# A decode kernel's single rows on fewer partitions, and ten small loads that nothing reads

## The chip, the core and the metric

The kernel runs on one core of a Trainium2 chip. Five engines work at once, each through its own list of instructions in order: TensorE (PE, with its weight loads PEld), VectorE (DVE), ScalarE (ACT), GpSimd (POOL) and SyncE (SP). Sixteen DMA engines move data between HBM and the on-chip memory; SP, ScalarE and GpSimd can issue transfers to them. The metric is the device time of one execution in microseconds.

## The reference

One token is decoded by an attention block with a cache of 32 heads, 4096 keys and 128 columns, and, beside it, by a gated feed-forward layer of 1376 hidden units. Both read the same normalized row `xn` of 512 numbers:

```python
xn = layernorm(x)
q = (xn @ wq).reshape(32 heads, 128)
p = softmax(q @ k_cache^T / sqrt(128))
a = (p @ v_cache).reshape(4096) @ wo
y = (silu(xn @ w_gate) * (xn @ w_up)) @ w_down * sigmoid(xn @ w_r)
out = x + a + xn + y
```

All of it is fp32. The two caches are 64 MB each; `wq` and `wo` are 8 MB, the three feed-forward matrices 2.7 MB each. Nothing is used twice.

## The kernel before, in words

The caches are worked off in eight groups of four heads. A group's keys and its values are 8 MB each, 64 KB on each of 128 partitions. Three regions take them in turn: `ring` holds three slots of half a group (and, beyond, some space for the feed-forward matrices), `vals` holds a whole group.

For each group DVE and POOL multiply the keys by q and add up along the columns (`multiply`, `sums`, `rest`; lines 253, 264, 269, 271), PE and DVE take the maximum of a head over the partitions, ScalarE takes the exponential (line 337), POOL spreads it into `PT[g % 2]` (line 339), and PE multiplies it with the values (line 348). In the loop over g (line 432 on) the keys of group g are loaded ahead of the values of group g-1, so that transfers run beside the work on the group before. At the end come `w_down`, and `wo` in parts that get smaller and smaller, so that little is left to do when the last one lands.

SP issues nearly all transfers, in the order of the program: `wq` (line 84), the single rows (line 133), the keys of group 0 (K0) into `vals`, the two halves of `w_gate` and the two of `w_up` (line 93), then, each when its place is free, K1, V0, K2, V1 and so on. ScalarE issues two loads of 2 KB at the start, x and `w_r` (lines 129 and 130). GpSimd issues none.

`w_down` has 1376 rows. The last 1344 are laid over 128 partitions in one piece (line 123). The first 32, the single rows, have a tile of their own, `WF` (lines 132 and 133): one row of 2 KB on each of 32 partitions, in an order that makes 4 (`FEW`) the leading dimension of the source. `ffn_hidden` (line 290 on) makes the hidden units, lays the first 32 beside the others as one more block of 32 columns in `hr`, transposes, and takes `HF`, one column of 32 units, from the result. `rows_down` (line 399 on) multiplies `HF` with `WF` in one matmul (line 405) behind those with the other rows. `q_part(0)` (line 283) makes the q of the first four groups: a matmul on PE and, as its last step, a copy on ScalarE (line 245). `PT[1]` is first written at group 1.

What sets the order of the work around the change is the framework's planner. Each engine's own order is that of the program (`manual_schedule`, line 69). The planner lays these orders side by side in one list, and counts the completions of transfers that SP and ScalarE issue on eight counters, handed out in turn along that list. A transfer whose counter has had an owner waits, on the engine that issues it, until that owner has landed, beside its waits for data. In the program as it was built before, the list begins so (number of the counter, and the former owner that is waited for):

```
x 0 | wq 1 | w_r 2 | single rows 3 | K0 4
... ScalarE's copy of q_part(0) (line 245)
w_gate, first half 5 | ... | w_gate, second half 6 | w_up, first half 7
w_up, second half 0 (x) | K1 1 (wq) | V0 2 (w_r) | K2 3 (single rows)
```

The first half of `w_gate` stands directly behind ScalarE's copy of line 245, and directly ahead of POOL's and DVE's first work on K0. GpSimd's transfers have counters of their own.

Of the kernel before, what the change touches and what calls it, by code (L numbers as in the profile page):

```python
# [8 lines left out]
F32 = mybir.dt.float32  # L9
AF = mybir.ActivationFunctionType  # L10
ALU = mybir.AluOpType
# [10 lines left out]
PARTS = (16,), (8, 4, 2.5, 1, 0.5)  # L22
T = 32
FEW = 4


@with_exitstack
def kernel(
# [13 lines left out]
    nc = tc.nc  # L42
    _, H, Sk, Dh = k_cache.shape
    D = x.shape[-1]
# [14 lines left out]
    NS = -(-QR // NCOL)  # L59
# [10 lines left out]
    const = ctx.enter_context(tc.tile_pool(name="const", bufs=1))  # L70
# [12 lines left out]
    def load_wq(t):  # L83
        nc.sync.dma_start(t, wq.rearrange("(p j) n -> p (j n)", p=P))  # L84

        return [
            t[:, j * H * Dh:(j + 1) * H * Dh].rearrange("p (b h k n) -> p b h k n", b=NB, h=HP, n=QC)
            for j in range(NK)
        ]
# [16 lines left out]
    def load_keys(g):  # L106

        i = (1 - g % 2) * SLOT
        t = load_group(k_cache, g, ring[:, i:i + 2 * SLOT] if g else vals)
        t = [t[:, :HC], t[:, HC:]]  # L110
        return [(h, t[h]) for h in ((1, 0) if g % 2 else (0, 1))]
# [17 lines left out]
    nc.scalar.dma_start(xr, x[0])  # L129
    nc.scalar.dma_start(wr, w_r.rearrange("(o n) -> o n", o=1))  # L130
    WQ = load_wq(ring[:, :2 * SLOT])
    WF = const.tile([T, D], F32, name="wf")
    nc.sync.dma_start(WF, w_down[:T].rearrange("(b a) n -> a b n", a=FEW))  # L133
    K, V = {0: load_keys(0)}, {}


# [42 lines left out]
    PT = [const.tile([P, C, HP], F32, name=f"pt{i}") for i in range(2)]  # L179
# [17 lines left out]
    for j in range(NK):  # L197
        nc.tensor.matmul(ps[:, j:j + 1], xn.rearrange("o (p j) -> o j p", j=NK)[:, j], ones[0:1, 0:1],  # L198
                         start=True, stop=True)
# [3 lines left out]
    def sigmoid(z, shape, name):  # L203
        e = const.tile(shape, F32, name=name)
        nc.scalar.activation(e, z, AF.Exp, scale=-1.0)
        nc.vector.tensor_scalar(e, e, 1.0, None, op0=ALU.add)
        nc.vector.reciprocal(e, e)
        return e
# [7 lines left out]
    sr = sigmoid(ps[:, 0:1], [P, 1], "sr")  # L216

    base = const.tile([1, D], F32, name="base")
# [5 lines left out]
    for j in range(NK):  # L224
        for i in range(NQ * HP):
# [3 lines left out]
                             start=(j == 0), stop=(j == NK - 1), skip_group_check=True)  # L229
# [7 lines left out]
    late = [ring[:, SLOTS * SLOT + i * D:SLOTS * SLOT + (i + 1) * D] for i in range(MORE // D)]  # L237

    def q_part(k):

        ps = ps_q.tile([P, QB, Dh], F32, name="q")
        nc.tensor.matmul(ps.rearrange("p g d -> p (g d)"), pick.rearrange("p i h -> p (i h)"), q_sb[:, k, :],
                         start=True, stop=True)

        nc.scalar.activation(q_sb[:, k, :], ps.rearrange("p g d -> p (g d)"), AF.Copy)
        return ps
# [4 lines left out]
    def multiply(g, i, c0, c1):  # L251
        q, k = Q[g // QB][:, g % QB, :], K[g][i][1]
        nc.vector.tensor_tensor(  # L253
            k[:, c0:c1, :], k[:, c0:c1, :],
            q[:, None, :].to_broadcast([P, c1 - c0, Dh]), op=ALU.mult
        )
# [9 lines left out]
    def rest(g, i):  # L266

        k, q = K[g][i][1][:, HC - NP:], q_sb[:, g // QB, :].rearrange("p (g d) -> p g d", d=Dh)[:, g % QB, :]
        nc.gpsimd.tensor_tensor(k, k, q[:, None, :].to_broadcast([P, NP, Dh]), op=ALU.mult)  # L269
        a, b = k[:, :, :Dh // 2], k[:, :, Dh // 2:]  # L270
        nc.gpsimd.tensor_tensor(a, a, b, op=ALU.add)  # L271


    def ffn_in(W, ps):

        for j in range(NK):
            for t in range(NCOL):
                a = 0 if t == 0 else T
                nc.tensor.matmul(ps[32 * t:32 * t + 1, a:T + FT], xnT[:, j:j + 1], W[j][:, t * FT + a:T + (t + 1) * FT],  # L279
                                 start=(j == 0), stop=(j == NK - 1), skip_group_check=True)  # L280
        return ps[:, :T + FT]

    Q = {0: q_part(0)}

    rest(0, 0)
    multiply(0, 0, 0, HC - NP)
    sums(0, 0)
    gate, up = ffn_in(W_GATE, ps_acc), ffn_in(W_UP, ps_o)

    def ffn_hidden():  # L290

        hid = sigmoid(gate, [P, T + FT], "hid")
        nc.vector.tensor_tensor(hid, hid, gate, op=ALU.mult)
        hr = late[3][:, :(NS + 2) * T].rearrange("p (s i) -> p s i", i=T)
        nc.vector.memset(hr[:, :NS + 1], 0.0)
        nc.vector.scalar_tensor_tensor(
            hr[:, NS + 1].rearrange("p (a b) -> p a b", a=FEW), hid[:, :T].rearrange("p (b a) -> p a b", a=FEW), sr,
            up[:, :T].rearrange("p (b a) -> p a b", a=FEW), op0=ALU.mult, op1=ALU.mult,
        )
        for a in range(HP):  # L300
            n = min(NS + 1, QR - OFF[a])
            nc.vector.scalar_tensor_tensor(
                hr.rearrange("p s (v a) -> p a s v", a=HP)[:, a, :n],
                hid[:, T:].rearrange("p (v r) -> p r v", r=QR)[:, OFF[a]:OFF[a] + n], sr,
                up[:, T:].rearrange("p (v r) -> p r v", r=QR)[:, OFF[a]:OFF[a] + n], op0=ALU.mult, op1=ALU.mult,
            )
        hT = late[4][:, :(NS + 2) * T].rearrange("p (s i) -> p s i", i=T)
        nc.vector.transpose(hT.rearrange("p s i -> p (s i)"), hr.rearrange("p s i -> p (s i)"))
        HL = const.tile([P, NS, 2, HP], F32, name="HL")
        for w in range(2):  # L310
            nc.vector.tensor_tensor(HL[:, :, w, :], hT[:, w:w + NS, 0:1].to_broadcast([P, NS, HP]),
                                    mine[:, None, :].to_broadcast([P, NS, HP]), op=ALU.mult)
        HF = const.tile([T, 1], F32, name="HF")
        nc.vector.tensor_copy(HF, hT[:T, NS + 1, 0:1])
        return HL, HF


# [81 lines left out]
    def rows_down():  # L399

        for s in range(NS):
            t, a, b = 32 * (s % NCOL), s * D, min((s + 1) * D, FP)
            nc.tensor.matmul(down[t:t + 2 * HP, :b - a], HL[:, s].rearrange("p w a -> p (w a)"), WD[:, a:b],
                             start=(s < NCOL), stop=(s >= NS - NCOL and t > 0), skip_group_check=True)
        nc.tensor.matmul(down[0:1, :], HF, WF, start=False, stop=True, skip_group_check=True)
        sb = small.tile([P, D], F32, name="sb")
        nc.scalar.activation(sb, down, AF.Copy)
        return sb
# [16 lines left out]
    def direct(lhsT, rhs, last=False):  # L425

        for j in range(NCOL):
            nc.tensor.matmul(fin(j), lhsT, rhs[:, j * DC:(j + 1) * DC],  # L428
                             start=False, stop=last, skip_group_check=True)


    for g in range(NG + 1):
# [3 lines left out]
        elif g:  # L436
# [6 lines left out]
            down = ps_q.tile([P, QB, Dh], F32, name="q").rearrange("p g d -> p (g d)")  # L443
# [5 lines left out]
        n = (HC - NP) // 2  # L449
# [17 lines left out]
        if g:  # L467
            values(g - 1)
            keep(g - 1)
            if g == 1:  # L470
                HL, HF = ffn_hidden()
            if g == NG:
                sb = rows_down()
            if g % GB == 0:
                DEN[g // GB - 1] = collect(g // GB - 1)
# [4 lines left out]
    n = len(rows) - RB + PARTS[1][0]  # L480
# [7 lines left out]
    for j, (lhsT, rhs) in enumerate(rows[n:]):  # L488
        if j == PARTS[1][1]:
            gather(sb, first[:, 0, 0, 0:1])  # L490
        direct(lhsT, rhs, last=(rhs is rows[-1][1]))
    res = const.tile([1, D], F32, name="res")
    for j in range(NCOL):
        to = res[:, j * DC:(j + 1) * DC]
        if j % 2:
# [32 lines left out]
```

## Time and profile before

| what | value |
|---|---|
| time, median of 2 runs | 376.82 us (376.81 to 376.84) |
| span of the profiled execution, first to last instruction | 375.2 us |
| bytes read from HBM | 159.45 MB |
| mean rate over the span | 425 GB/s |
| DMA packets | 3826, of them 455 under 512 B |
| mean granted clock of TensorE | 0.686 |

The time of the profiled execution itself is not given beside its span; the two runs agree to 0.03 us, and the span is 1.6 us shorter than their median.

How to read the views quoted below. The page's first part has the busy time of each engine and its share of the span; its second part cuts the span in 40 slices and gives the busy share in tenths; its third has the DMA queues with packets, megabytes and share of 16 engines; its fourth follows the chain of work that ended last back through whatever released each step. The timeline has start, duration, engine, line, operation, what is written and read, and in brackets the idle time before and what ended it. SPq and ACTq are issues of transfers. The DMA view of a stretch gives its busy share and GB/s in 40 slices; a packet is counted where it starts. Packets under 512 B are, before the change, completion marks: one from each DMA engine that took part in a transfer.

### The profile page before, as it was taken

How to read it: one execution, taken by the hardware profiler on the slowest of the kernel's cores; microseconds unless marked ns; L12 is line 12 of the kernel's file. 1: busy time of each engine (PE TensorE's matmuls, PEld its weight loads, DVE VectorE, ACT ScalarE, POOL GpSimd, SP SyncE). 2: the span in 40 equal slices, each digit the busy share in tenths (PEclk: the TensorE clock that was granted, in tenths of full speed). 3: DMA queues.
4: the chain of work that ended last, by engine and by line, in shares of the span. 5: the costliest groups of instructions: out<-in, count | busy, mean ns of one | idle time of the engine just before them, and what ended most of it. 6: DMA issues, size and time to landing. Idle time of an engine off the chain costs nothing.

```text
span 375.2 us, 2071 instructions
## 1 busy us (share of the span) xinstructions
PE 117.0 (31%) x850; PEld 34.7 (9%) x850; DVE 228.4 (61%) x132; ACT 16.1 (4%) x37; POOL 172.1 (46%) x56
## 2 busy tenths in 40 slices
PE   1155052000810074006400480037002700180996
PEld 1111010000200011001100130001000200020222
DVE  6300499389867990699059924995399419970020
ACT  3001000000010000100000000000000000010001
POOL 2000497089307940696059704980299019910000
PEclk9999567555775559555955596558555865586799
DMA  8999899999999999999999999999999999998995
GB/s 336 447 454 447 363 462 442 447 447 426 433 412 413 447 449 426 447 440 426 433 412 433 447 442 426 447 440 421 426 434 433 447 419 433 447 435 387 441 416 226
DMA packets 3826, 159.57 MB, mean 425 GB/s; under 512 B 455, under 2 KB 583, under 8 KB 874
## 3 DMA queue, kind: packets, MB, share of 16 engines
q1 hardware_dynamic: 3814, 159.45, 98.5%
q8 instruction: 6, 0.10, 0.1%
q14 instruction: 2, 0.02, 0.0%
q10 hardware_dynamic: 4, 0.00, 0.0%
HBM read 159.45 MB, written 0.00 MB: 425 GB/s over the span
## 4 chain that ended last, share of the span: by engine, by line
DMA 74%; PE 17%; DVE 7%; SPq 1%; issue 0%; ACTq 0%; ACT 0%; DVEq 0%
DMA vals<-in_A_v_cache_dram 54%; PE ps_pv L348 17%; DMA vals<-in_A_k_cache_dram 11%; DMA ring<-in_A_wo_dram 9%; DVE s L264 4%; DVE vals L253 3%; SPq L133 0%; PE ps_acc L428 0%; SPq L118 0%; PE ps_small L324 0%; SPq L84 0%; ACTq L523 0%; ACT res L496 0%; DVE nm L329 0%; PE ps_o L428 0%
## 5 line engine op out<-in xcount | busy, mean ns | idle before, releaser
L269 POOL TENSOR_TENSOR ring<-ring,q_sb 128x3072 f32<-128x3072 f32 x14 | 93.6, 6683 | 116.4 <-DMA ring<-in_A_k_cache_dram 116.4
L348 PE MATMUL ps_pv<-vals,pt 128*16 128x512 f32 x448 | 63.8, 734 | 187.3 <-DMA vals<-in_A_v_cache_dram 187.3
L253 DVE TENSOR_TENSOR ring<-ring,q 128x2560 f32<-128x2560 f32 (+1 forms) x21 | 77.8, 3703 | 71.4 <-DMA ring<-in_A_k_cache_dram 71.4
L264 DVE TENSOR_REDUCE s<-ring 128x40 f32<-128x5120 f32 (+1 forms) x28 | 100.0, 3614 | 0.8
L271 POOL TENSOR_TENSOR ring<-ring 128x1536 f32<-128x1536 f32 x14 | 48.1, 3435 | 1.1
L348 PEld LDWEIGHTS ps_pv<-vals,pt 128*16 128x16 f32 x448 | 15.1, 113 | 231.1 <-issue 231.1
L269 POOL TENSOR_TENSOR vals<-vals,q_sb 128x3072 f32<-128x3072 f32 x2 | 13.4, 6708 | 37.7 <-DMA vals<-in_A_k_cache_dram 37.7
L253 DVE TENSOR_TENSOR vals<-vals,q 128x5120 f32<-128x5120 f32 x2 | 11.0, 5483 | 28.4 <-DMA vals<-in_A_k_cache_dram 28.4
L373 DVE RECIPROCAL rinv<-ps_small 128x4 f32<-128x4 f32 x2 | 0.4, 178 | 23.2 <-PE ps_small L364 23.2
L264 DVE TENSOR_REDUCE s<-vals 128x40 f32<-128x5120 f32 (+1 forms) x4 | 14.3, 3614 | 0.1
L357 ACT ACTIVATE pv<-ps_pv 128x512 f32<-128x512 f32 x8 | 4.8, 597 | 193.9 <-PE ps_pv L348 193.9
L348 PE MATMUL ps_pv<-ring,pt 128*16 128x512 f32 x64 | 9.3, 746 | 10.3 <-DMA ring<-in_A_v_cache_dram 10.3
L227 PE MATMUL ps_pv<-ring,xnT 128*1 128x512 f32 x64 | 8.8, 712 | 10.5 <-DMA ring<-in_A_wq_dram 10.5
L339 POOL TENSOR_TENSOR pt<-e,mine 128x512 f32<-128x512 f32 x8 | 8.3, 1040 | 7.9 <-ACT e L337 7.9
L279 PE MATMUL ps_acc<-ring,xnT 128*1 128x336 f32 (+1 forms) x32 | 4.9, 766 | 16.5 <-DMA ring<-in_B_w_gate_dram 16.5
L324 PE MATMUL ps_small<-dg,same 128*128 128x32 f32 x16 | 3.6, 309 | 18.1 <-DVE dg L322 18.1
L337 ACT ACTIVATE e<-s,nm 128x128 f32<-128x128 f32 x8 | 3.2, 402 | 119.3 <-DVE nm L329 119.3
L366 PE MATMUL ps_o<-pv,first 128*128 128x512 f32 x16 | 7.4, 604 | 0.4 <-ACT pv L357 0.4
L271 POOL TENSOR_TENSOR vals<-vals 128x1536 f32<-128x1536 f32 x2 | 6.9, 3444 | 0.2
L324 PEld LDWEIGHTS ps_small<-dg,same 128*128 128x128 f32 x16 | 2.9, 218 | 24.4 <-issue 14.9
L198 PE MATMUL ps_small<-ones,pv 1*128 1x1 f32 x8 | 2.0, 370 | 8.3 <-DVE pv L194 8.3
L375 DVE TENSOR_TENSOR ring<-ps_o,rinv 128x512 f32<-128x512 f32 x2 | 2.1, 1058 | 3.4 <-PE ps_o L366 3.4
(106 smaller groups left out, 82.5 us busy)
## 6 DMA issues: line engine op xcount, KB each, us to landing
vals<-in_A_wo_dram SPq DMA_DIRECT2D x1, 4096.0 KB, 26.4
ring<-in_B_w_gate_dram SPq DMA_DIRECT2D x2, 1376.0 KB, 44.7
ring<-in_B_w_up_dram SPq DMA_DIRECT2D x2, 1376.0 KB
vals<-in_B_w_down_dram SPq DMA_DIRECT2D x1, 2688.0 KB
ring<-in_A_wo_dram SPq DMA_DIRECT2D x1, 2048.0 KB
ring<-in_A_wo_dram SPq DMA_DIRECT2D x1, 1024.0 KB
ring<-in_A_wo_dram SPq DMA_DIRECT2D x1, 640.0 KB, 34.2
ring<-in_A_wo_dram SPq DMA_DIRECT2D x1, 256.0 KB, 34.3
```

The costliest lines, as they stand in the source:

```text
L227: nc.tensor.matmul(ps_pv[i // NCOL][32 * t:32 * t + 1, :QC], xnT[:, j:j + 1], WQ[j][:, k * QB // GB, i % HP, k % (GB // QB), :], start=(j ...
L253: nc.vector.tensor_tensor(k[:, c0:c1, :], k[:, c0:c1, :], q[:, None, :].to_broadcast([P, c1 - c0, Dh]), op=ALU.mult)
L264: nc.vector.tensor_reduce(s[:, c], k[:, c, :n], axis=AX.X, op=ALU.add)
L269: nc.gpsimd.tensor_tensor(k, k, q[:, None, :].to_broadcast([P, NP, Dh]), op=ALU.mult)
L271: nc.gpsimd.tensor_tensor(a, a, b, op=ALU.add)
L279: nc.tensor.matmul(ps[32 * t:32 * t + 1, a:T + FT], xnT[:, j:j + 1], W[j][:, t * FT + a:T + (t + 1) * FT], start=(j == 0), stop=(j == NK - ...
L324: nc.tensor.matmul(ps[:, :PP], same.rearrange("p i h -> p (i h)"), dg, start=True, stop=True)
L337: nc.scalar.activation(e, s, AF.Exp, bias=nm, scale=SCALE, accum_out=RS[g // GB][:, g % GB:g % GB + 1])
L339: nc.gpsimd.tensor_tensor(PT[g % 2], e[:, :, None].to_broadcast([P, C, HP]), mine[:, None, :].to_broadcast([P, C, HP]), op=ALU.mult)
L348: nc.tensor.matmul(ps[r:r + M, :], p[:, G * i:G * (i + 1), :].rearrange("p c h -> p (c h)"), v[:, G * i:G * (i + 1), :].rearrange("p c d - ...
L357: nc.scalar.activation(PV[g // GB][:, :, g % GB, :], ps_pv[g % 2].rearrange("p (c d) -> p c d", c=G), AF.Copy)
L366: nc.tensor.matmul(ps_o, first[:, c].rearrange("p h i -> p (h i)"), pv[:, c].rearrange("p k d -> p (k d)"), start=(c == 0), stop=(c == G - 1))
```

## The change

The single rows go onto 16 partitions, two consecutive rows (4 KB) on each; the leading dimension of the source stays 4. `hr` and `hT` get one more block of 32 columns, the first 32 units are laid as two blocks of 16, `HF` becomes two columns of 16 units, and two matmuls over 16 rows take the place of one over 32. The result row `res` uses the tile `base`, which has been read by then, instead of its own. And behind `q_part(0)` ScalarE issues seven loads of 5 to 11 rows of 128 B, GpSimd three of 5, 5 and 4 rows of 256, 192 and 160 B, all from `wo` into columns of `PT[1]` that are disjoint. Nothing reads them; `PT[1]` is overwritten as a whole at group 1.

```diff
+EACH = 2
@@ load of the single rows
-    WF = const.tile([T, D], F32, name="wf")
-    nc.sync.dma_start(WF, w_down[:T].rearrange("(b a) n -> a b n", a=FEW))
+    WF = const.tile([T // EACH, EACH * D], F32, name="wf")
+    nc.sync.dma_start(WF, w_down[:T].rearrange("(a b r) n -> a b (r n)", a=FEW, r=EACH))
@@ behind Q = {0: q_part(0)}, ahead of rest(0, 0)
+    mark, x = PT[1].rearrange("p c h -> p (c h)"), 0
+    for n in (5, 6, 7, 8, 9, 10, 11):
+        nc.scalar.dma_start(mark[:n, x:x + T], wo[16 * n:17 * n, :T])
+        x += T
+    for n, w in ((5, 64), (5, 48), (4, 40)):
+        nc.gpsimd.dma_start(mark[:n, x:x + w], wo[16 * n:17 * n, :w])
+        x += w
@@ ffn_hidden
-        hr = late[3][:, :(NS + 2) * T].rearrange("p (s i) -> p s i", i=T)
-        nc.vector.memset(hr[:, :NS + 1], 0.0)
+        hr = late[3][:, :(NS + 1 + EACH) * T].rearrange("p (s i) -> p s i", i=T)
+        nc.vector.memset(hr, 0.0)
         nc.vector.scalar_tensor_tensor(
-            hr[:, NS + 1].rearrange("p (a b) -> p a b", a=FEW), hid[:, :T].rearrange("p (b a) -> p a b", a=FEW), sr,
-            up[:, :T].rearrange("p (b a) -> p a b", a=FEW), op0=ALU.mult, op1=ALU.mult,
+            hr[:, NS + 1:, :T // EACH], hid[:, :T].rearrange("p (i r) -> p r i", r=EACH), sr,
+            up[:, :T].rearrange("p (i r) -> p r i", r=EACH), op0=ALU.mult, op1=ALU.mult,
         )
...
-        hT = late[4][:, :(NS + 2) * T].rearrange("p (s i) -> p s i", i=T)
+        hT = late[4][:, :(NS + 1 + EACH) * T].rearrange("p (s i) -> p s i", i=T)
...
-        HF = const.tile([T, 1], F32, name="HF")
-        nc.vector.tensor_copy(HF, hT[:T, NS + 1, 0:1])
+        HF = const.tile([T // EACH, EACH, 1], F32, name="HF")
+        nc.vector.tensor_copy(HF, hT[:T // EACH, NS + 1:, 0:1])
@@ rows_down
-        nc.tensor.matmul(down[0:1, :], HF, WF, start=False, stop=True, skip_group_check=True)
+        for r in range(EACH):
+            nc.tensor.matmul(down[0:1, :], HF[:, r], WF[:, r * D:(r + 1) * D], start=False, stop=(r == EACH - 1),
+                             skip_group_check=True)
@@ the end
-    res = const.tile([1, D], F32, name="res")
+    res = base
```

## The prediction

> **What bounds the kernel now.** I read the page from its second part down, then the chain of waits, then the timeline around the place of the edit, then the DMA view in narrow stretches. From the page:
>
> ```profile
> PE 117.0 (31%) x850; PEld 34.7 (9%) x850; DVE 228.4 (61%) x132; ACT 16.1 (4%) x37; POOL 172.1 (46%) x56
> DMA  8999899999999999999999999999999999998995
> q1 hardware_dynamic: 3814, 159.45, 98.5%
> DMA 74%; PE 17%; DVE 7%; SPq 1%; issue 0%; ACTq 0%; ACT 0%; DVEq 0%
> ```
>
> No engine is busy for more than 61% of the span; the 16 DMA engines are for 98.5%, with 159.45 MB on the one queue of SP. Its windows say the same for the long middle (last two numbers: share of the 16 engines, GB/s):
>
> ```profile
> 73.60:344.00 270.40, 71.26 (x474) 19.44 (x474) 190.25 (x90) 8.98 (x25) 149.38 (x36) 0.63 1.00 435
> ```
>
> The chain of waits agrees at the end: the last piece of wo takes from its issue to 371.40 us, and 3.8 us of small work follow.
>
> ```profile
> 337.19 34.21 DMA ring<-in_A_wo_dram
> 371.40 0.04 issue
> ```
>
> So the span is bytes divided by 435 GB/s, plus whatever time a DMA engine stands empty or is made to do more. An edit matters if it does one of these two to the engine that ends last, and otherwise not. The profiled execution spans 375.2 us; the runs shown have a median of 376.82, so 1.6 us lie around the span, which I leave as they are.
>
> **The place of the edit.** The timeline of the first 60 us (start, duration, engine; SPq and ACTq are issues):
>
> ```profile
> 0.73 0.52 ACTq L129 DMA_DIRECT2D pv<-in_A_x_dram  x1
> 0.73 0.41 SPq L84 DMA_DIRECT2D ring<-in_A_wq_dram  x1
> 1.21 0.80 SPq L133 DMA_DIRECT2D wf<-in_B_w_down_dram  x1
> 1.28 0.21 ACTq L130 DMA_DIRECT2D pv<-in_B_w_r_dram  x1
> 2.06 0.59 SPq L103 DMA_DIRECT2D vals<-in_A_k_cache_dram  x1
> 2.69 1.23 SPq L93 DMA_DIRECT2D ring<-in_B_w_gate_dram  x2
> 3.96 1.26 SPq L93 DMA_DIRECT2D ring<-in_B_w_up_dram  x2
> 4.74 0.47 POOL L178 TENSOR_TENSOR turned<-first 128x1 f32<-128x1 f32 x3 [1.88 <-DVE first L173]
> 31.97 0.56 SPq L103 DMA_DIRECT2D ring<-in_A_k_cache_dram  x1
> 32.99 0.60 ACT L245 ACTIVATE q_sb<-q 128x512 f32<-128x512 f32 x1 [0.42 <-PE q L242]
> 42.88 5.49 DVE L253 TENSOR_TENSOR vals<-vals,q 128x5120 f32<-128x5120 f32 x1 [28.42 <-DMA vals<-in_A_k_cache_dram]
> 42.92 6.69 POOL L269 TENSOR_TENSOR vals<-vals,q_sb 128x3072 f32<-128x3072 f32 x1 [37.71 <-DMA vals<-in_A_k_cache_dram]
> ```
>
> SP issues wq, the single rows, K of group 0 and the four halves of w_gate and w_up within the first 5.2 us. That is what keeps the DMA engines fed until K1, issued at 31.97.
>
> **Part 1, the single rows.** Before: 32 pieces of 2 KB on four engines, 16 KB each. After: 16 pieces of 4 KB on the same four (the leading dimension stays 4). Bytes are unchanged; a few gaps between pieces go. I take 0, bounds -0.1 and +0.1 us.
>
> **Part 2, a second matmul against them.** L405 is one fp32 matmul, in two passes; after there are two of these.
>
> ```profile
> 358.19 1.01 PE L405 MATMUL q<-wf,HF 32*1 32x512 f32 x2
> 359.24 0.60 ACT L407 ACTIVATE sb<-q 128x512 f32<-128x512 f32 x1 [2.89 <-PE q L405]
> 362.98 0.11 PEld L387 LDWEIGHTS q<-vals,ring 128*1 128x1 f32 x8 [0.76 <-DMA vals<-in_A_wo_dram]
> 367.26 0.14 PEld L387 LDWEIGHTS q<-ring 128*1 128x1 f32 x8 [1.60 <-issue]
> 368.15 0.40 PE L414 MATMUL ps_small<-sb,turned 128*32 128x128 f32 x8
> ```
>
> That is +1.0 us of PE at 358. Of it 0.76 is covered by the wait for wo ahead of L387; the other 0.24 disappears in the 1.60 us ahead of the second L387 group. ScalarE's copy L407 ends 1.0 later, at 360.8, and L414 reads it at 368.15. Cost 0; without the cover, 1.0. On DVE the memset and the transpose get 64 and 32 columns more:
>
> ```profile
> L308 DVE STREAM_TRANSPOSE ring<-ring 128x416 f32<-128x416 f32 x1 | 0.6, 611 | 0.0
> L295 DVE MEMSET ring<- 128x384 f32 x1 | 0.4, 378 | 0.0
> L253 DVE TENSOR_TENSOR ring<-ring,q 128x2560 f32<-128x2560 f32 (+1 forms) x3 | 11.1, 3702 | 3.0 <-DMA ring<-in_A_k_cache_dram 3.0
> ```
>
> By length 0.05 + 0.06 us, ahead of a wait of 3.0 us for K. Cost 0. Using base for res removes a tile and orders nothing new that is late.
>
> **Part 3, GpSimd's three loads.** They stand behind L178, so they issue at about 5.2 us; POOL has nothing until 42.92 (37.71 idle). Nobody reads them. The cover is enough for issues of up to 12 us each; their bytes (under 4 KB) are nothing. It would be gone if these loads had to wait for ScalarE's, which go to the same tile:
>
> ```profile
> 68.15 0.55 SPq L103 DMA_DIRECT2D vals<-in_A_v_cache_dram  x1
> 75.97 2.82 DVE L253 TENSOR_TENSOR ring<-ring,q 128x2560 f32<-128x2560 f32 x1 [7.25 <-DMA ring<-in_A_k_cache_dram]
> 373.17 0.28 SPq L499 DMA_DIRECT2D out_dram<-res  x1
> ```
>
> The 2 KB store at the end is through 2.0 us after its issue (373.17 to 375.2). Ten such steps behind 33.6 end at 54; L269 in order behind them, and V0, which waits for what L269 reads, come 11 us late. V0's issue moves to 79, its first packets to 80.9 at the latest (1.7 from issue to packet, Part 5), and K1 is through at 75.97: 4.9 us, 381.7. But the columns are disjoint, and the halves of w_gate go to one tile 0.6 us apart without a wait. Cost 0.
>
> **Part 4, what seven loads on ScalarE cost the DMA engines.** They stand behind L245, so they issue from 33.6. ScalarE's next work comes 45.34 us later:
>
> ```profile
> 78.92 0.40 ACT L337 ACTIVATE e<-s,nm 128x128 f32<-128x128 f32 x1 [45.34 <-DVE nm L329]
> ```
>
> Seven issues of 0.2 to 0.5 us are hidden there. On the DMA engines the nearest rows are the two 2 KB loads of ScalarE, in the DMA view of 0 to 12 us (40 slices of 0.3 us):
>
> ```profile
> GB/s 0 0 0 0 0 881 2185 437 0 0 0 0 0 0 0 218 1529 1529 218 0 0 0 0 218 1311 1754 218 0 0 0 0 218 1092 1966 218 0 0 0 0 0
> q10 hardware_dynamic: 4, 0.00, 0.3%
> ```
>
> Four packets (two loads, two completion marks) took 0.3% of 16 engines for 12 us, 0.58 us, so 0.29 a load at most, the cold start included. The busiest engine meets eight of the ten loads: 2.3 us as an upper end; by bytes alone (128 B, against 2 KB) nearly 0. I take 0.1, since only the first was cold.
>
> **Part 5, what they do to SP's order.** This term decides. The planner counts the transfers of SP and ScalarE on eight counters, handed out in turn in planned order, and lets each wait until the former owner of its counter has landed (the kernel section has the list). Before, that hurts nowhere: the last w_up half waits for x, V0 for w_r. In the planned list of before the first w_gate half stands directly behind L245's copy. The seven loads follow that copy on ScalarE, and by the trace they need 1.5 to 3.6 us from 33.6, against 8.7 until K0 lands, where the planner seems to place the first w_gate half. So I expect all seven ahead of it. They then take counters 5, 6, 7, 0, 1, 2, 3, and the first half of w_gate gets counter 4, that of K0: it may not be issued before K0 has landed. Behind it on SP's queue wait the second half, both of w_up, and K1.
>
> ```profile
> 2.06 40.73 DMA vals<-in_A_k_cache_dram
> ```
>
> K0's landing reaches the waiting engines at 42.79, instead of an issue at 2.69. By then nothing is queued. How long the engines stand empty follows from two more readings. In the view of 0 to 12 us, wq's first packets begin 1.5 to 2.4 us into the span, 0.8 to 1.7 after the issue at 0.73; the next begin 3.0 later, later ones every 2.4, so the first took 0.6 longer. And w_gate's packets now begin from 41.25 (first full slice of the view of 41 to 43 us, 0.05 us each) to 42.35 (the last of K0's sixteen marks, the packet under 512 B, is within 42.30 to 42.40):
>
> ```profile
> GB/s 0 0 0 0 0 440 440 0 440 440 440 440 440 881 440 0 440 0 0 0 440 881 881 440 440 440 881 440 440 881 440 0 440 0 0 0 440 440 440 1321
> DMA packets 49, 0.73 MB, mean 363 GB/s; under 512 B 16, under 2 KB 16, under 8 KB 16
> DMA packets 4, 0.07 MB, mean 661 GB/s; under 512 B 1, under 2 KB 1, under 8 KB 1
> ```
>
> After: 42.79 + 0.8 to 1.7 = 43.6 to 44.5, middle 44.05, against a middle of 41.8: 2.25 us of emptiness for an average engine (2.15 between the last ones). The first packets' extra lies between 0 (the engines are warm) and 0.6 (as at the start); I take the middle, 0.3, neither row being nearer. 2.25 + 0.3 = 2.55. Part 4 then costs nothing, since the loads are through before the restart.
>
> The Trainium skill, page DMA: Bandwidth & Descriptors, section Specifications, gives about 0.6 us from a SyncE issue to the first byte. By that estimate the engines would restart near 43.4 and the sum would be 378.4. The trace shows 0.8 to 1.7, and the measurement decides.
>
> The queue holds no slack to win this back: with a share of 1.00 from 73.6 to 344 us, a shift passes straight to 371.40. Sum: 0 + 0 + 0 + 2.5, so a span of 377.7 and a time of 376.8 + 2.5 = 379.3.
>
> **Rivals.**
> No drain: the planner mixes the loads with w_gate's and w_up's halves, so that none of SP's transfers inherits K0 or the one just ahead of it. For it: the list shows an order, not distances. Then Part 4 alone counts: 376.8 + 0.1 = 376.9.
> Faster: the drain restarts all engines together or the loads hold back the ones ahead, so that the last engine does less. One engine is held by each fetch of instructions (view of 56 to 60 us), 1.6% of 16 engines for 4 us, 1.0 us:
>
> ```profile
> q8 instruction: 1, 0.02, 1.6%
> ```
>
> If one such delay misses the last engine and nothing drains: 376.8 - 1.0 = 375.8. Against it: the loads add work and move no fetch.
> Slower by over 2%: every small load stops its DMA engine for as long as a fetch of instructions does, 1.0 us by the row above. The engine that meets eight of them ends 8.2 us late, and K0's landing, the restart and the end with it: 376.8 + 8.2 = 385.0 without a drain, 387.5 with one. It decides from 0.95 us a load (7.5 us in all). Against it: the 0.58 us of two whole loads in Part 4.
>
> **Chances.** Drain once, 0.63; no drain, 0.28; faster, 0.05; POOL late or loads that stop their engines, 0.04, of which 0.03 over 2%. The forecast is the first, by itself 378.6 (a restart 0.8 after the wait for all: 43.6 - 41.8 = 1.8) to 380.6 (44.5 + 0.6 against an early engine's 41.25, 3.8). To hold eight in ten the range takes in no drain too, with Part 4 at 0 and Part 1 at its lower bound (376.7): 376.6 to 380.6. A measurement of this kernel can tell about 2%, 7.5 us, from no change; both main cases lie within. Slower by more: 0.03. Faster by more, which no case gives: 0.01. The rest, 0.96, is within.
>
> **What would show it.** Right: SP's issues of w_gate move from 2.69 to about 42.8 and K1's to about 45; the DMA row of the page has a dip in its slice 5, q10 has 7 loads more, wo's last piece lands near 374. Wrong: w_gate still issued before 6 us and a share near 1.0 between 41 and 46 us (no drain), or V0's issue later than 70 us with a dip behind 73 (POOL late, or another counter). L387 starting more than 0.3 us behind wo's landing would break Part 2. What would undo the forecast is a planned order in which fewer than seven loads stand together between two of SP's transfers.

## The result, and the profile after

| kernel | time, median | span of its executions | outside the span |
|---|---|---|---|
| before, beside the changed one | 376.82 us (376.81 to 376.84, 2 runs) | 375.2 (the profiled one) | not given run by run |
| changed | 380.81 us (380.68, 380.94) | 378.6, 378.9 | 2.1, 2.0 |
| before, in a repetition | 376.92 us (11 runs) | 374.9 to 375.3 | 1.8 |
| changed, in the repetition | 380.77 us (380.50 to 381.16, 4 runs) | 378.6 to 379.2 | 1.9 to 2.0 |

The ratio is 1.0103 with a 95% interval of 1.0086 to 1.0119; in the repetition 1.0103 (1.0090 to 1.0116). So the change costs 3.9 us. That is within 2%, but it is clear of the noise, as the interval leaves out 1, and it lies 0.2 us above the range of the prediction. Three executions of the experiments below, two of the kernel before and one of rows_only, were in a slower state (387.5 to 400.2 us) and are left out of all ratios.

The changed kernel's page has these lines in its second and third parts. The fifth figure of the DMA row (slice 5, 37.9 to 47.3 us) has fallen from 8 to 6, and SP's queue q1 has lost 0.7 points of its share. Of the small traffic, q10 (ScalarE's loads) has grown from 4 packets to 116, and q0 (GpSimd's loads) is new.

```profile
DMA  8999699999999999999999999999999999998995
...
q1 hardware_dynamic: 3810, 159.45, 97.8%
...
q10 hardware_dynamic: 116, 0.01, 0.0%
q0 software_dynamic: 96, 0.00, 0.0%
```

The changed kernel's timeline of the first 60 us shows why (start, duration, engine, line; its lines stand one to eleven further down than before):

```profile
1.20 0.41 SPq L134 DMA_DIRECT2D wf<-in_B_w_down_dram  x1
1.66 0.61 SPq L104 DMA_DIRECT2D vals<-in_A_k_cache_dram  x1
...
42.68 1.14 SPq L94 DMA_DIRECT2D ring<-in_B_w_gate_dram  x2
43.86 1.23 SPq L94 DMA_DIRECT2D ring<-in_B_w_up_dram  x2
45.22 0.55 SPq L104 DMA_DIRECT2D ring<-in_A_k_cache_dram  x1
```

SP's issues of `w_gate` have moved from 2.69 to 42.68, and K1's from 31.97 to 45.22. The list of waits of the changed kernel, SP alone (us in total, times, longest), names what SP waited for: K0. It goes to `vals`, while `w_gate` goes to `ring`, so this is no wait for data or for a place.

```profile
SPq L94 <- DMA vals<-in_A_k_cache_dram: 40.4, 1, 40.4
```

The chain of waits of the changed kernel now runs through that place, and its last transfer lands at 340.77 + 33.92 = 374.69, 3.3 us later than before (371.40):

```profile
1.66 41.00 DMA vals<-in_A_k_cache_dram
42.66 0.02 issue
42.68 0.49 SPq L94
...
45.22 33.79 DMA ring<-in_A_k_cache_dram
...
340.77 33.92 DMA ring<-in_A_wo_dram
```

How much was lost there is read from the windows of 40 to 50 us (the last three numbers: granted clock, share of the DMA engines, GB/s). First the kernel before, then the changed one:

```profile
40.00:50.00 10.00, 0.58 (x8) 0.20 (x12) 7.09 (x2) 0.00 (x0) 7.00 (x2) 0.50 0.88 376
```

```profile
40.00:50.00 10.00, 0.00 (x0) 0.00 (x0) 7.21 (x2) 0.00 (x0) 7.12 (x2) 0.50 0.64 247
```

At the 435 GB/s of the long middle the missing rate is (376 - 247) x 10 / 435 = 3.0 us. The 3.3 us by which the last transfer lands later show that nothing behind it gives this back.

### The profile page after: what moved, and what is told of

Its sections match the earlier page's. It is cut to its first block, busy times and chain, and to the rows that moved or that the text cites. A ratio compares the mean times of both kernels' runs of the same rounds, so it can differ in the third digit from the quotient of the medians.

```text
span 378.6 us, 2090 instructions
## 1 busy us (share of the span) xinstructions
PE 118.5 (31%) x852; PEld 35.0 (9%) x852; DVE 228.5 (60%) x132; ACT 16.1 (4%) x37; POOL 173.9 (46%) x59
## 4 chain that ended last, share of the span: by engine, by line
DMA 71%; DVE 21%; PE 5%; SPq 1%; issue 0%; ACTq 0%; ACT 0%; DVEq 0%
DMA ring<-in_A_k_cache_dram 36%; DMA vals<-in_A_v_cache_dram 16%; DVE s L265 11%; DMA vals<-in_A_k_cache_dram 11%; DMA ring<-in_A_wo_dram 9%; DVE ring L254 9%; PE ps_pv L357 5%; SPq L94 1%; DVE ring L384 0%; PE ps_acc L439 0%; SPq L119 0%; DVE ring L390 0%; DVE nm L338 0%; PE ps_small L333 0%; SPq L134 0%
## 5 line engine op out<-in xcount | busy, mean ns | idle before, releaser
L357 PE MATMUL ps_pv<-vals,pt 128*16 128x512 f32 x448 | 62.9, 725 | 191.5 <-DMA vals<-in_A_v_cache_dram 191.5
L280 PE MATMUL ps_o<-ring,xnT 128*1 128x336 f32 (+1 forms) x32 | 4.0, 643 | 1.4 <-DMA ring<-in_B_w_up_dram 1.4
```

The source lines that it names most:

```text
L357: nc.tensor.matmul(ps[r:r + M, :], p[:, G * i:G * (i + 1), :].rearrange("p c h -> p (c h)"), v[:, G * i:G * (i + 1), :].rearrange("p c d - ...
```

## The experiments

Fourteen kernels were run, each in five rounds against the kernel before on the same chip, with 4 to 11 executions each. The theory: a transfer of SP, the first half of `w_gate`, inherits the completion counter of K0 and so waits for K0; meanwhile the DMA engines run out of work (this is called the drain). Its rivals: the ten loads cost the time themselves, or the rows' new layout does. What is listed are medians, and the ratio to the kernel before with its 95% interval.

| kernel | rows | loads of ScalarE + GpSimd | time, us | ratio |
|---|---|---|---|---|
| rows_only | on 16 DMA engines | 0 + 0 | 377.17 | 1.0005 (0.9996 to 1.0014) |
| rows_4 | on 4 | 0 + 0 | 376.85 | 1.0000 (0.9992 to 1.0009) |
| gp_only | as before | 0 + 3 | 376.99 | 1.0003 (0.9994 to 1.0012) |
| no_gp | on 16 | 7 + 0 | 380.75 | 1.0107 (1.0093 to 1.0120) |
| one_row7 | on 16 | 7 of one row + 3 | 380.99 | 1.0129 (1.0101 to 1.0157) |
| early7 | on 16 | 7, placed early, + 3 | 377.49 | 1.0017 (1.0008 to 1.0026) |
| acts5 | on 16 | 5 + 3 | 377.41 | 1.0015 (1.0007 to 1.0024) |
| acts6 | on 16 | 6 + 3 | 377.53 | 1.0017 (1.0008 to 1.0025) |
| acts8 | on 16 | 8 + 3 | 379.45 | 1.0066 (1.0042 to 1.0091) |
| acts15 | on 16 | 15 + 3 | 381.83 | 1.0127 (1.0112 to 1.0142) |
| after_rows4 | on 4 | 7 + 3 | 380.52 | 1.0099 (1.0082 to 1.0116) |
| six_rows4 | on 4 | 6 + 3 | 379.30 | 1.0068 (1.0056 to 1.0080) |
| five_rows4 | on 4 | 5 + 3 | 377.12 | 1.0006 (0.9997 to 1.0015) |
| after_again | on 16 | 7 + 3 | 380.77 | 1.0103 (1.0090 to 1.0116) |

**Six and eight loads instead of seven.** The edit only changes the list of lengths; acts6 has the first of the two lists, acts8 the second:

```diff
-    for n in (5, 6, 7, 8, 9, 10, 11):
+    for n in (5, 6, 7, 8, 9, 10):
```

```diff
-    for n in (5, 6, 7, 8, 9, 10, 11):
+    for n in (5, 6, 7, 8, 9, 10, 11, 12):
```

> Six small loads on ScalarE instead of seven; all else as changed. Drain theory: every later counter moves by one, the first half of w_gate gets the counter of the single rows, which land near 22.4, so SP issues it near 22.5, behind K0 in the queue; only the second half waits for K0, with the 1.4 MB of the first half in the queue. The dip behind 41 goes, the last piece of wo lands 3.0 to 3.4 us earlier than in the changed kernel, near 372.0, and the time falls from 380.8 to 377.3 to 377.9. Load theory (the small loads and their completion marks cost the time themselves): one load of seven less gives back at most 0.6, 380.2 or more.

One load less gives back 3.2 us (380.77 to 377.53), five times the 0.6 that one load may cost by the load theory. In the list of waits of acts6 (SP alone) the wait is split: the first half of `w_gate` waits for the single rows, and only the second for K0.

```profile
SPq L94 <- DMA wf<-in_B_w_down_dram: 21.1, 1, 21.1
SPq L94 <- DMA vals<-in_A_k_cache_dram: 18.7, 1, 18.7
```

```profile
40.00:50.00 10.00, 0.77 (x8) 0.31 (x12) 7.25 (x2) 0.00 (x0) 7.16 (x2) 0.50 0.88 375
```

The window above, of acts6, is back at the rate of before (376).

> Eight small loads on ScalarE instead of seven, the eighth of 12 rows; all else as changed. Drain theory: the first half of w_gate gets the counter of the first small load, which landed between 36.8 and 42.2 in the changed kernel; SP issues it before K0 is through, so the dip goes or shrinks: 377.3 to 378.9. Load theory: one load more costs 0 to 0.6, 380.8 to 381.4.

With one load more the time falls too, by 1.3 us, which the load theory excludes; but the median lies above what was expected, and the runs scatter from 377.81 to 380.58. Its list of waits and its timeline show where the issue stands now:

```profile
SPq L94 <- DMA pt<-in_A_wo_dram: 40.0, 2, 37.9
40.21 3.09 SPq L94 DMA_DIRECT2D ring<-in_B_w_gate_dram  x2
```

The first half waits for the first small load (`pt`) and goes out at 40.21. By the single packets of the trace the first DMA engine is through with K0 at 41.60, so the issue comes only just in time. In the profiled run the drain is short; that it is longer in the longer ones would explain the scatter, but only that one run has a trace.

**The same seven loads elsewhere.** early7 moves them ahead of ScalarE's first computation:

```diff
     PT = [const.tile([P, C, HP], F32, name=f"pt{i}") for i in range(2)]
+    mark, x = PT[1].rearrange("p c h -> p (c h)"), 0
+    for n in (5, 6, 7, 8, 9, 10, 11):
+        nc.scalar.dma_start(mark[:n, x:x + T], wo[16 * n:17 * n, :T])
+        x += T
```

> The same seven loads on ScalarE, of the same rows into the same columns, but ahead of its first computation instead of behind the copy of q; GpSimd's three stay. In the planned list they now stand ahead of the single rows and K0, so K0 gets the counter of the first load and the first half of w_gate that of the second, both landed within some us of the start. Drain theory: no dip behind 41, 377.3 to 377.8, as with six loads. Load theory (the loads cost the time, wherever their counters stand): 380.5 or more. ScalarE's seventh load waits for wq near 22.5 and holds back the normalization of x behind it; if q came too late for K0 at 42.8, the dip would be on DVE and K1 later, 378 to 380.

```profile
20.24 3.79 SPq L94 DMA_DIRECT2D ring<-in_B_w_gate_dram  x2
```

377.49: the same loads, of the same bytes, without the 3.3 us. The line above is from its timeline: `w_gate` is issued at 20.24, long before K0 is through. The normalization, which came later now, as was feared, cost nothing that can be seen beside the 377.41 of acts5 (below). What the loads do depends on where they stand in the planned list.

**Loads without their bytes, and without GpSimd's.** one_row7 cuts each of ScalarE's loads to one row:

```diff
-        nc.scalar.dma_start(mark[:n, x:x + T], wo[16 * n:17 * n, :T])
+        nc.scalar.dma_start(mark[:1, x:x + T], wo[16 * n:16 * n + 1, :T])
```

> The changed kernel with each of ScalarE's seven loads cut to one row of 128 B, seven packets of data instead of 56. Drain theory: what counts is how many transfers stand there, so the drain stays and the time is 380.3 to 380.8, the lower end if the data packets cost some tenths. Theory that the packets of the loads cost the time: 377.5 to 378.5.

```profile
q10 hardware_dynamic: 18, 0.01, 0.0%
```

380.99, nothing gained (0.2 above the upper end), and the drain is still there. The line above, from its page, shows that this edit took away more than data: q10 has 18 packets instead of 116. By the single packets, ScalarE's loads now have 7 packets of data instead of 56, and 7 completion marks instead of 56 as well. So the bulk of the loads' packets of both kinds is not what costs the 3.4 us. Some tenths can't be told here: two of the six runs took 383.55 and 383.68, for a reason that no trace shows. no_gp takes the three GpSimd loads out of the changed kernel, and gp_only puts the same three lines alone into the kernel before, behind `q_part(0)`:

```diff
-    for n, w in ((5, 64), (5, 48), (4, 40)):
-        nc.gpsimd.dma_start(mark[:n, x:x + w], wo[16 * n:17 * n, :w])
-        x += w
```

> The changed kernel without GpSimd's three loads. The drain stays in both theories (span near 378.6). Theory that GpSimd's queue is what adds 0.6 us outside the span (2.2 of 380.8, against 1.6 before): 380.2, with 1.6 outside the span. Rival (the 0.6 comes with something else, such as where the last fetch of instructions falls): 380.6 to 381.0, still 2.0 to 2.2 outside.

> The kernel before with GpSimd's three loads alone. If they cost nothing, as the changed kernel without them suggests: 376.8 to 377.0. If they carry the 0.36 us by which the kernel with six loads on ScalarE and three on GpSimd stands above the rows alone: 377.2.

380.75 and 376.99. GpSimd's loads cost between nothing and 0.1 us. The theory that they lengthen the time outside the span falls: it is still 1.9 to 2.1 us in no_gp. The 0.6 us of it was mostly a false comparison, one execution's span (375.2) against the median time of others; run by run the kernel before has 1.8 outside its span.

**The rows alone, and which DMA engines carry them.** rows_only is the changed kernel without the ten loads:

```diff
-    mark, x = PT[1].rearrange("p c h -> p (c h)"), 0
-    for n in (5, 6, 7, 8, 9, 10, 11):
...
-    for n, w in ((5, 64), (5, 48), (4, 40)):
...
```

> The single rows on 16 partitions, the two matmuls and the shared result tile alone, without any small load. If the rows cost nothing: 376.7 to 376.9. If their new spread over all 16 DMA engines (about 0.16 us on each, instead of about 0.65 on four) delays the engine that ends last: 377.0. If the second matmul were on the path to the end: 377.8. No dip behind 41 in any of them.

377.17. By itself the 0.28 us above 376.89 can't be told from nothing (the interval holds 1), but it comes back below. In the DMA view of 21.5 to 23 us of rows_only 32 packets are completion marks:

```profile
DMA packets 64, 1.11 MB, mean 743 GB/s; under 512 B 32, under 2 KB 32, under 8 KB 48
```

Before, the same view has 20:

```profile
DMA packets 68, 1.11 MB, mean 743 GB/s; under 512 B 20, under 2 KB 20, under 8 KB 52
```

16 of each are those of `wq`. So the single rows leave 16 marks now, not 4: they are on all 16 DMA engines, one piece of 4 KB each. rows_4 keeps 4 as the leading dimension by another order of the source, with the units laid out to match:

```diff
-    nc.sync.dma_start(WF, w_down[:T].rearrange("(a b r) n -> a b (r n)", a=FEW, r=EACH))
+    nc.sync.dma_start(WF, w_down[:T].rearrange("(b a r) n -> a b (r n)", a=FEW, r=EACH))
```

> The kernel with the rows alone (no small loads), but with the source taken in the order in which 4 stays the leading dimension of the transfer, and the units laid out to match by two instructions instead of one. Theory of the spread (4 KB on every one of 16 DMA engines delays the one that ends last, 16 KB on four do not): 376.8 to 377.0, and the packets of the single rows on four engines. Rival (the 0.28 us of the rows alone come from the second matmul or the shared result tile): 377.1 to 377.3.

```profile
DMA packets 52, 1.11 MB, mean 743 GB/s; under 512 B 20, under 2 KB 20, under 8 KB 36
```

The line above is the same view of rows_4: 20 marks, four engines, and 376.85 us, with the two matmuls and the shared tile still there. Three pairs that differ only in this order and the layout that goes with it (after_rows4, six_rows4 and five_rows4 are rows_4 with the loads put back, seven, six and five on ScalarE and three on GpSimd) give the spread's price: 377.17 - 376.85 = 0.32, 380.77 - 380.52 = 0.25 (after_again and after_rows4) and 377.41 - 377.12 = 0.29 (acts5 and five_rows4). The first and the third rest on 11 runs a kernel; the second has four a kernel, which overlap, and would not show it alone.

> The changed kernel, all ten loads kept, but with the single rows taken in the order that keeps 4 the leading dimension. If the spread's 0.3 us and the drain's are independent terms of one sum: 380.4 to 380.6. If the drain evens out the DMA engines, so that the spread no longer matters: 380.8.

> The changed kernel itself, unaltered, since its time so far rests on two runs: 380.5 to 381.0 in every theory. It is the base for the differences of the other kernels.

**A longer wait.** acts15 gives the first half of `w_gate` the counter of the eighth load, which itself waits for K0 (each load is cut to 64 B a row, so that the columns fit):

```diff
-    for n in (5, 6, 7, 8, 9, 10, 11):
-        nc.scalar.dma_start(mark[:n, x:x + T], wo[16 * n:17 * n, :T])
-        x += T
+    for n in 2 * (5, 6, 7, 8, 9, 10, 11) + (12,):
+        nc.scalar.dma_start(mark[:n, x:x + T // 2], wo[16 * n:17 * n, :T // 2])
+        x += T // 2
```

> Fifteen loads on ScalarE, each of 64 B a row; GpSimd's three stay. The eighth gets K0's counter and waits for K0 itself; the first half of w_gate gets the eighth load's counter and so waits for one more trip through the DMA engines, issued near 42.7 and landed some 1.6 to 2.2 us later (the store at the end needs 2.0). Drain theory: w_gate's first issue at 44.3 to 45, the emptiness grows by that and passes to the end whole: 382.4 to 383.3. Rival (a drain costs a fixed amount that the queues behind it partly win back): below 382. Load theory (eight loads more at what six to seven seem to cost, 0.25 us): 381.1.

```profile
SPq L94 <- DMA pt<-in_A_wo_dram: 41.7, 1, 41.7
43.98 1.13 SPq L94 DMA_DIRECT2D ring<-in_B_w_gate_dram  x2
```

The wait is now for a small load (`pt`), as the theory has it. The issue is 1.30 us later than in the changed kernel (43.98 in this timeline against 42.68), and the span is 1.3 us longer (medians of 380.05 and 378.75). So in the span the shift passes to the end whole. The expected time was missed, for one part because a small load's way through empty DMA engines took 1.3 us, not 1.6 to 2.2. The time, 381.83, rose by only 1.06 and so lies below 382, where the rival expected it; it is the span that speaks against the rival, as the part outside the span was 1.8 here and 2.0 in the changed kernel. Why that part differs is not known. The DMA view of 43.5 to 45.5 us of acts15 (40 slices of 0.05 us) also shows that SP's restart was no quicker while small loads ran on the DMA engines:

```profile
GB/s 0 4 3 0 0 0 0 0 3 5 0 0 0 0 0 4 3 3 0 0 0 0 7 1 0 3 0 0 0 8 3 1 0 0 0 2642 881 881 1321 0
```

Small loads run through the whole stretch, and `w_gate` starts in the 36th slice, at 45.25, 1.27 us behind its issue; in the changed kernel it is 1.27 too (below).

**Where the sum did not hold.** six_rows4 joins what two kernels had shown harmless: six loads, and the rows on four engines.

> Six loads on ScalarE, GpSimd's three, and the single rows in the order that keeps 4 the leading dimension: both costs found so far are taken out, and only the loads themselves are left, 0.36 us by the difference of two earlier kernels. If the terms add: 376.9 + 0.36 = 377.2 to 377.3. If the loads' share was part of the spread's: 376.9 to 377.0.

379.30, 2.1 us too much. The window of 40 to 50 us of six_rows4 has lost rate again:

```profile
40.00:50.00 10.00, 0.00 (x0) 0.00 (x0) 7.29 (x2) 0.00 (x0) 7.21 (x2) 0.50 0.85 324
```

The second half of `w_gate` waits for all of K0, here as in acts6, and until its packets come an engine has only the first half to do: 1376 KB / 16 engines = 86 KB (88 thousand bytes), 3.2 us at 435 / 16 = 27.2 GB/s an engine. Where the single rows burden only four engines, the other twelve are through with K0 earlier. The DMA views of 41 to 43 us show it (a non-zero slice is one in which a packet of `w_gate` starts), first acts6, then six_rows4:

```profile
GB/s 0 0 0 0 0 0 0 0 0 443 889 440 446 883 881 443 1324 0 443 440 0 440 0 0 0 0 881 883 440 881 881 0 1761 0 440 0 440 440 0 0
```

```profile
GB/s 443 443 0 443 0 881 441 443 886 881 0 440 0 0 0 443 0 881 0 1326 0 1324 440 440 440 881 440 0 440 0 0 440 0 443 443 0 1321 881 440 881
```

In acts6 the first engine turns to `w_gate` at 41.45 and has work until 44.7; in six_rows4 at about 41.0, until 44.3. The timeline of six_rows4 has the second half's issue at its end:

```profile
23.06 20.02 SPq L94 DMA_DIRECT2D ring<-in_B_w_gate_dram  x2
```

Two issues end at 43.08, so with about 0.5 us for one the second begins near 42.6, and after a restart of 1.27 us its first packets could come near 43.9. The single packets of the trace show them on the last engines only at 46.3: between 44.4 and 46.4 up to seven of the sixteen engines stand empty, 0.5 us of all sixteen, and many packets take longer than the usual 0.82 us. The missing rate of the window, (375 - 324) x 10 / 435 = 1.2 us, holds both. So it is shown that the order of the rows tips this kernel into a drain that acts6 escapes, though both issue the second half at about the same time (42.64 and 42.59). Why its packets come up to 3.7 us behind the issue here, and where the rest of the 2.1 us goes, is not shown. With five loads, in five_rows4 as in acts5, the wait falls on the first half of `w_up`, and twice as much lies ahead of it:

```diff
-    for n in (5, 6, 7, 8, 9, 10):
+    for n in (5, 6, 7, 8, 9):
```

> As the kernel with six loads and 4 as the leading dimension (379.3), but with five loads. The counters move by one more: both halves of w_gate get counters whose owners land by 22.5, and only the first half of w_up waits for K0, with twice as much queued ahead of it (eight packets of 0.82 us on an engine, 6.5 us, instead of four). Partial-drain theory: no engine runs dry behind 44, the rate of 40 to 50 us is back at 365 to 380 GB/s (324 with six), and the time is 377.1 to 377.4. Rival (the 2.1 us come from the order of the rows together with the loads, whatever is queued): 379 or more.

```profile
40.00:50.00 10.00, 0.83 (x8) 0.31 (x12) 7.32 (x2) 0.00 (x0) 7.23 (x2) 0.50 0.89 381
```

The window above is that of five_rows4: full rate, and 377.12 us. So the wait as such is harmless; what counts, by these kernels, is how much the engines have queued while the last one lets SP go.

> The changed kernel with five loads on ScalarE instead of seven, the rows spread as changed. If the kernel with six (377.5) held a small rest of the drain: 377.2 to 377.35, and what the loads themselves cost shrinks from 0.36 to 0.1 to 0.2. If it held none: 377.4 to 377.6.

377.41, at the lower edge of the second expectation: six loads held at most 0.1 us of a drain. Without any drain the eight loads then cost 377.41 - 377.17 = 0.24 us (acts5 against rows_only), or 377.12 - 376.85 = 0.27 (five_rows4 against rows_4).

## Why the prediction was right and where it failed

Against 376.9 before, the runs split the 3.9 us into three steps: 0.3 for the spread of the rows (rows_only), 0.25 for eight loads without a drain (acts5), and 3.4 for the drain (380.77 - 377.41 = 3.36, and on four engines 380.52 - 377.12 = 3.40). As steps from one kernel to the next they add up to 3.95 by construction; what supports the split is that the kernels on four engines give the same steps for the loads (0.27) and the drain. That the loads cost their 0.25 also in the drained kernel is assumed; loads and drain together are 380.77 - 377.17 = 3.6.

**Part 5, the mechanism, was right.** The counter of K0, the move of `w_gate` to 42.68 (forecast 42.8) and of K1 to 45.22 (45), the dip in slice 5, and an undiminished shift to the end all came as forecast; acts6, early7 and one_row7 show that it is the counter and not the loads, and in acts15 an owner that lands later makes the shift longer.

**Part 5, the size, failed:** the term of 2.55 measured 3.4. Of its two parts the emptiness (2.25) was a little too small and the first packets' extra (0.3) by half or more. The DMA view of the changed kernel from 43.5 to 45.5 us:

```profile
GB/s 0 0 0 0 0 0 0 0 0 1761 440 881 440 881 0 440 0 440 0 0 440 0 881 0 440 0 0 0 0 0 0 0 0 0 0 0 0 0 0 1321
DMA packets 19, 0.42 MB, mean 209 GB/s; under 512 B 0, under 2 KB 0, under 8 KB 0
```

The sixteen first packets start from 43.95 to 44.75, 1.27 to 2.05 behind the issue at 42.68, where 43.6 to 44.5 was forecast from the start of the kernel. (There the 0.8 was read from the start of a slice of 0.3 us; by the single packets the first of wq began at 1.77, 1.04 behind its issue.) The next start in the last slice, from 45.45: a first packet takes up to 1.5 us and more, and by the rate of the long middle 22 KB are 0.8. The single packets of the trace put it at 1.39 on average against 0.82, so the first packets' extra is 0.57, not 0.3; the row of the kernel's start (0.6) was the right one of the two bounds. The argument for less, that the engines are warm, found no support in acts15: there small loads ran up to the restart, and the first packets still took 1.50 on average. From the end of K0's last packets (41.91 on average) to the first packets' start (44.23) are 2.3, and with 0.57 that is 2.9, near the 3.0 of the window. The same reckoning in the other traces with the same drain gives 2.47 + 0.65 = 3.1 in after_again, 2.49 + 0.72 = 3.2 in no_gp, 2.40 + 0.69 = 3.1 in after_rows4 and 2.19 + 0.81 = 3.0 in one_row7. So the drain is about 3.1 us, and the medians of the spans differ by as much (378.75 in after_again, 375.6 in acts5). The other 0.2 of the 3.36 lie outside the span (2.0 against 1.85 in acts5); why that part grows stays open.

The prediction cited the Trainium skill, page DMA: Bandwidth & Descriptors, section Specifications, with some 0.6 us from an issue to the first byte. The trace shows 1.27 at the earliest engine, and the sum of 378.4 by that estimate is 2.4 too low.

**Part 1 failed** with 16 pieces "on the same four": the two outer dimensions of the new source lie contiguously, and the rows went to 16 engines. So the leading dimension did not stay 4, though the section on the change says so too. Its 0 (bounds of 0.1) is 0.25 to 0.32. A piece of 4 KB on every engine explains about 0.15 of it (an estimate: 64 KB took 2.4); the other half has no row. The same page of the Trainium skill, section "Why a DMA increments its semaphore by 16 and not by 1", says that the number of engines is the largest, up to 16, that divides the slowest dimension of both sides, as the instruction carries them. The marks agree with that if the instruction carries the merged 16, and 16 marks are what the trace has.

**Part 2 and Part 3 were right:** rows_4 has the second matmul and the shared tile at no cost, and GpSimd's loads delayed nothing. **Part 4** took 0.1 for the loads without a drain and nothing beside one; without a drain all of them together cost 0.25. By the single packets a packet of 128 B takes 13 ns and a mark 9 ns, so an engine that meets all seven loads gives 7 x 22 = 154 ns to them, an estimate of 0.15 us. What the rest is stays open, and no run tries the marks by themselves.

**The part outside the span** was left as 1.6 on both sides. Run by run it was 1.8 before and 2.0 after, and this growth adds 0.2 to the miss. The upper end of the range, 380.6, held the drain at its worst, but with Part 1, Part 4 and the growth of this part at nothing, and these are some 0.7 together. Of the rivals, "no drain" did not happen; acts5 shows that its 376.9 would have been 377.4 for the same reasons.

## What to carry to other kernels

A transfer that nothing reads can still stop another queue, through the counter that it hands on: count the transfers between two issues in the planned order, and look for the owner eight places earlier. A wait behind a long load cost nothing where each DMA engine had enough queued: 3.2 us was just enough with six loads and too little when the first engines ended half a microsecond earlier, 6.5 us was enough (acts6, six_rows4, five_rows4). Where the queues ran dry, the emptiness showed up at the end undiminished, as the DMA engines were busy all the way behind it. Two changes that are each harmless can use up the same reserve, so run the combination.

## What the runs showed of the hardware

- A restart on empty DMA queues took 1.27 to 2.05 us from the issue to an engine's first packet, and that packet took 1.39 us on average instead of 0.82. Small loads of another queue on the same engines made neither shorter (acts15: 1.27 for the first, 1.50 on average).
- Sixteen rows taken as four times four contiguous ones went to sixteen DMA engines; in an order that keeps the four apart they went to four. The wider spread was 0.25 to 0.32 us slower; why is not shown beyond the 4 KB that every engine then has to move.
- A small load of ScalarE, issued when K0 had landed, released a wait 1.30 us later (acts15), against 2.0 us from the issue of the 2 KB store to the end of the span in the kernel before.
